# A sparse-attention and two-layer expert kernel: the experts' first layer as seven block products on two of three token chunks

## The chip, the cores and the metric

The kernel runs on one core of a Trainium2 chip. The metric is the device time of one execution in microseconds (us); the median of a few runs is quoted. A profiled execution is a run of its own, with a time of its own and a span from its first to its last instruction.

## The reference

Attention (2 batches, 8 heads, 768 positions, head size 64, each query sees 4 sink positions and a window of 128) gives 1536 tokens of 512 numbers. A first feed-forward part follows, and then four weighted experts, which are dense: every token goes through every expert.

```python
x = attention(q, k, v)                      # [1536, 512]
h = x @ w_in                                # [512, 2048]
g = np.maximum(h, 0.0) + alpha * np.minimum(h, 0.0)
y = g @ w_out                               # [2048, 512]
p = domain_probs / (domain_probs.sum(-1, keepdims=True) + 1e-09)
for e in range(4):
    h = np.maximum(y @ w1[e], 0.0)          # w1[e] [512, 1024]
    out += p[:, e:e + 1] * (h @ w2[e])      # w2[e] [1024, 512]
```

## The kernel before, in words

Every fp32 operand of the feed-forward parts is split into a high part (fp32r, what TensorE takes) and a low part (the rest), and a product is three matmuls: high by high, high by low, low by high. A matmul takes 128x128 weights and a moving tile of 512 columns.

Tokens come in three chunks `c` of 512 (`CH`). Hidden features come in f-tiles of 128: 16 of the first part (`N1`), then 8 for each expert, 48 in all (`NW`), numbered `k` or `f`. An f-tile's weights are four 128x128 blocks of the first layer and 512 columns of the second, together 1024 columns, held as `wh` (high) and `wl` (low), loaded in two halves of 512 columns into four raw buffers `wraw` and split by ScalarE (L119, high) and GpSimd or VectorE (L121, low). Eight f-tiles fit at a time: six in the pool `work`, two in the pools `late`. `tick` starts one half and takes every half that is in flight a step further; `load_due` issues the loads that have become possible.

`fast` does the attention and, woven into it, the first f-tiles. `rest` does all that follows: a list of steps (block, chunk, f-tile). In a step TensorE runs `s1` (first layer: 12 matmuls into a PSUM bank, L201 to L203), then ScalarE and VectorE make the high part `hh` and the low part `hl` of the activation (`relu`, L239 and L240), and two steps later TensorE runs the second layer for that f-tile (`s2_natural`, L219 to L221: four token tiles of three matmuls each, into four PSUM banks which add up over the 8 f-tiles of an expert). At the end of a chunk of an expert VectorE multiplies each bank by the token's share and adds it to `acc` (L669), 12 times for each expert. In the last expert, each such row of 128 tokens is sent out (L671). `y` (in `xh`, `xl`) is what the first part leaves in `acc`, split (L659, L660).

Each engine works through its queue in the order of the program, and waits on semaphores. VectorE, ScalarE and GpSimd are fed by the same loop, so what stands ahead of an instruction in this order on its engine comes first.

Of the kernel before, what the change touches and what calls it, by code (L numbers as in the profile page):

```python
# [30 lines left out]
BLOCKS = [(0, 6), (6, 5), (11, 5)] + [(N1 + 8 * e, 8) for e in range(E)]  # L31
SW = 2 * P + SK
KW = 3 * P + 2 * SK
SLOTS, EARLY, RAW = 8, 6, 4
# [18 lines left out]
class Body:  # L53
# [37 lines left out]
    def half(self, j):  # L91

        nc, (k, i) = self.nc, divmod(j, 2)
        w = self.wraw.pop(j)
        if k < N1:
            top, low = w[:, :, 1], w[:, :, 0]
            m = self.work.tile([P, CH], I32, tag="cm", name=f"cm{j}", bufs=2)  # L100
            nc.scalar.activation(m.bitcast(F32), top.bitcast(F32), AF.Abs, scale=2.0 ** -112)
            if j not in DVE_LOW:
                nc.scalar.activation(low, low.bitcast(U32), AF.Copy, scale=2.0 ** -29)
            yield
            if j in DVE_LOW:
                nc.vector.tensor_scalar(low, low.bitcast(U32), 2.0 ** -29, None, ALU.mult)
            nc.vector.tensor_scalar(top, top, -0x80000000, None, ALU.bitwise_and)  # L107
            nc.vector.scalar_tensor_tensor(top, m, 3, top, ALU.logical_shift_left, ALU.bitwise_or)
            nc.gpsimd.tensor_tensor(top, top, low, ALU.add)
            yield  # L110
            w = top.bitcast(F32)
        if i == 0:
            slot = k % SLOTS - EARLY
# [8 lines left out]
        self.due.append(j + RAW)  # L122

    def tick(self, more=True):

        if self.queue and more:
            j = self.queue.pop(0)
            self.flight.append((j, self.half(j)))
# [94 lines left out]
    def prelu(self, pool, ps, n, col, name):  # L223

        nc = self.nc
        gh = pool.tile([P, n], F32R, tag="gh", name=f"gh{name}", bufs=3)
        gl = pool.tile([P, n], F32R, tag="gl", name=f"gl{name}", bufs=3)
        g = pool.tile([P, n], F32, tag="g", name=f"g{name}", bufs=2)
# [6 lines left out]
    def relu(self, pool, ps, n, name):  # L235
        nc = self.nc
        hh = pool.tile([P, n], F32R, tag="gh", name=f"hh{name}", bufs=3)
        hl = pool.tile([P, n], F32R, tag="gl", name=f"hl{name}", bufs=3)
        nc.scalar.activation(hh, ps, AF.Relu)  # L239
        nc.vector.scalar_tensor_tensor(hl, ps, 0.0, hh.bitcast(F32), ALU.max, ALU.subtract)  # L240
        return hh, hl


    def positions(self):
# [239 lines left out]
    def ahead(self):  # L484

        self.qk, self.v, self.vs, self.sp, self.ps, self.p = {}, {}, {}, {}, {}, {}
        self.den, self.pt, self.st, self.pv, self.nmax = {}, {}, {}, {}, {}
        self.r, self.rb, self.xf = {}, {}, {}
        self.xh, self.xl, self.acc = {}, {}, {}
        self.queue, self.flight, self.due = [], [], list(range(RAW))  # L490
        for j in range(3):
            self.at_load(j)

    def fast(self):
        nc, tc = self.nc, self.tc
        self.work = accp = tc.alloc_tile_pool(name="accp", bufs=1)
        for c in range(NC):
            self.acc[c] = accp.tile([P, 4, CH], F32, name=f"acc{c}")
        tmp = tc.alloc_tile_pool(name="tmp", bufs=1)
        psb = self.psb = tc.alloc_tile_pool(name="psb", bufs=1, space=PSUM)  # L500
        with tc.tile_pool(name="psa", bufs=1, space=PSUM) as self.psa:
            at = self.at = tc.alloc_tile_pool(name="at", bufs=1)
            self.atk = tc.alloc_tile_pool(name="atk", bufs=1, side="right")
            self.late = []
            for j in range(3, QK):
# [6 lines left out]
            for i, visits in enumerate(LEAD):  # L512
                steps = [(u, f, f == f0, f == f1 - 1) for u, f0, f1 in visits for f in range(f0, f1)]
# [7 lines left out]
            gs, outs, seen = {}, None, set()  # L521
            for p in range(NP + 4):
# [56 lines left out]
                if p % 2 == 0:  # L579
                    self.at_x(p - 4)  # L580
                if p == NP + 3:
                    at.release()
                    self.add_late()
                self.tick(p in STARTS)
# [6 lines left out]
        psb.release()  # L591
        for late in self.late[::-1]:
            late.release()
        tmp.release()
        accp.release()

    def add_late(self):
# [4 lines left out]
    def rest(self, pool, units, blk0):  # L602

        nc, tc = self.nc, self.tc
        n1 = len(BLOCKS) - E
# [5 lines left out]
        nxt = SLOTS  # L611
        with tc.tile_pool(name="psc", bufs=1, space=PSUM) as psc:
            psum = [self.psb, psc]
            gs, outs = {}, None
            for i in range(len(steps) + 2):
                if i < len(steps):
                    k, c, n, f = steps[i]
                    nn = n.stop - n.start
                    self.load_due()
                    ps = psum[i % 2].tile([P, CH], F32, tag="h", name=f"h{k}_{c}_{f}", bufs=2)[:, :nn]  # L620
                    self.ready(f)
                    self.s1(f, self.xh[c][:, :, n], self.xl[c][:, :, n], ps)
                    gs[i] = (self.prelu(pool, ps, nn, f, f"{c}_{f}") if k < n1
                             else self.relu(pool, ps, nn, f"{c}_{f}"))
# [18 lines left out]
                while nxt < NW and last.get(nxt - SLOTS, -1) <= i:  # L643
                    self.plan(nxt)
                    nxt += 1
                self.tick()
                if f < f1:
                    continue
                if k == n1 - 1:
                    self.new_x(c, "y")  # L650
                for d in range(4):
                    acc = self.acc[c][:, d, n]
                    if k == 0:
                        nc.vector.tensor_copy(acc, outs[d])
                        continue
                    if k < n1:
                        nc.vector.tensor_tensor(acc, outs[d], acc, ALU.add)
                        if k == n1 - 1:
# [7 lines left out]
                    if k == n1:  # L666
                        nc.vector.tensor_scalar(acc, outs[d], pr, None, ALU.mult)
                    else:
                        nc.vector.scalar_tensor_tensor(acc, outs[d], pr, acc, ALU.mult, ALU.add)  # L669
                    if k == len(BLOCKS) - 1:  # L670
                        nc.sync.dma_start(self.a["out"][nt * P:(nt + 1) * P, :], acc)  # L671


    def general(self):
# [146 lines left out]
```

## Time and profile before

| | |
|---|---|
| median of 3 runs | 933.68 us (932.7 to 934.55) |
| the profiled execution, its own time | 937.81 us |
| its span | 936.0 us |
| TensorE matmuls | 4760, busy for 98% of the span |
| VectorE, ScalarE, GpSimd busy | 38%, 30%, 29% |
| mean granted TensorE clock | 0.987 of full speed |

Busy times of TensorE overlap, since a matmul starts before the one ahead of it has ended; how fast it goes is read from the starts. The experts' first matmul starts its weight load at 397.17 us, and the last matmul of all starts at 929.43 us.

### The profile page before, as it was taken

What the parts mean: (1) busy time and instruction counts of PE and PEld (TensorE: products, weight loads), DVE (VectorE), ACT (ScalarE), POOL (GpSimd) and SP (SyncE); (2) the same over time, 40 slices, a digit from 0 to 9 for tenths busy, and PEclk for the clock granted to TensorE, in tenths of its full rate; (3) what the DMA queues carried; (4) which work ended last, traced back from release to release, by engine and by line L of the source; (5) the groups of instructions that cost most, each with busy time, mean ns of one, the idle gap of its engine ahead of it and who ended that gap; (6) DMA issues with size and microseconds to landing.
All of it is one profiled execution on the core that took longest, in us unless ns stands there. A gap on an engine that the chain in (4) does not pass through costs nothing.

```text
span 936.0 us, 12192 instructions
## 1 busy us (share of the span) xinstructions
PE 920.7 (98%) x4760; PEld 761.3 (81%) x4760; DVE 360.2 (38%) x770; ACT 285.3 (30%) x666; POOL 276.1 (29%) x250
## 2 busy tenths in 40 slices
PE   8999999998999999999999999999999999999997
PEld 5678899998878888888888888888888888888885
DVE  5678867647994634321212122121212121212121
ACT  4687766754431222321111221112121112211110
POOL 2366644535662554551001231002230012220000
PEclk9799999998999999999999999999999999999999
DMA  6554432202331020011001120001120001101011
GB/s 181 156 180 149 149 116 86 74 1 74 130 116 43 23 68 23 23 55 36 1 0 35 46 68 34 0 1 46 50 86 0 1 19 49 57 12 46 1 46 49
DMA packets 23715, 54.44 MB, mean 58 GB/s; under 512 B 3168, under 2 KB 3168, under 8 KB 23648
## 3 DMA queue, kind: packets, MB, share of 16 engines
q1 hardware_dynamic: 23504, 53.57, 17.7%
q8 instruction: 39, 0.64, 0.3%
q14 instruction: 28, 0.23, 0.1%
q10 hardware_dynamic: 144, 0.00, 0.0%
HBM read 50.42 MB, written 3.15 MB: 57 GB/s over the span
## 4 chain that ended last, share of the span: by engine, by line
PE 90%; DVE 7%; ACT 1%; issue 1%; POOL 0%; ACTq 0%; DVEq 0%; POOLq 0%
PE h L201 13%; PE h L202 13%; PE h L203 13%; PE o L221 9%; PE o L220 9%; PE o L219 9%; PE o L210 4%; PE o L211 4%; PE o L212 4%; PE pv L455 3%; PE s L348 2%; PE pt L408 2%; PE busy L184 1%; DVE wraw L107 1%; DVE wl L121 1%
## 5 line engine op out<-in xcount | busy, mean ns | idle before, releaser
L240 DVE SCALAR_TENSOR_TENSOR hl<-h,hh 128x512 fp32r<-128x512 f32 x96 | 66.4, 692 | 428.7 <-ACT hh L239 428.7
L121 POOL TENSOR_TENSOR wl<-wraw,wh 128x512 fp32r<-128x512 f32 x79 | 103.4, 1313 | 362.0 <-ACT wh L119 362.0
L239 ACT ACTIVATE hh<-h 128x512 fp32r<-128x512 f32 x96 | 57.4, 598 | 428.4 <-PE h L203 428.4
L202 PE MATMUL h<-yl,wh 128*128 128x512 f32 x384 | 150.2, 391 | 0.0
L221 PE MATMUL o<-wh,hl 128*128 128x512 f32 x384 | 150.2, 391 | 0.0
L201 PE MATMUL h<-yh,wh 128*128 128x512 f32 x384 | 150.2, 391 | 0.0
L219 PE MATMUL o<-wh,hh 128*128 128x512 f32 x384 | 150.0, 391 | 0.0
L220 PE MATMUL o<-wl,hh 128*128 128x512 f32 x384 | 150.0, 391 | 0.0
L203 PE MATMUL h<-yh,wl 128*128 128x512 f32 x384 | 149.8, 390 | 0.0
L201 PE MATMUL h<-xh,wh 128*128 128x256 f32 (+1 forms) x264 | 90.7, 344 | 0.0
L203 PE MATMUL h<-xh,wl 128*128 128x256 f32 (+1 forms) x264 | 88.3, 334 | 0.0
L202 PE MATMUL h<-xl,wh 128*128 128x256 f32 (+1 forms) x264 | 88.2, 334 | 0.0
L201 PEld LDWEIGHTS h<-yh,wh 128*128 128x128 f32 x384 | 72.0, 188 | 15.9
L203 PEld LDWEIGHTS h<-yh,wl 128*128 128x128 f32 x384 | 72.1, 188 | 15.8
L202 PEld LDWEIGHTS h<-yl,wh 128*128 128x128 f32 x384 | 72.1, 188 | 15.8
L221 PEld LDWEIGHTS o<-wh,hl 128*128 128x128 f32 x384 | 72.1, 188 | 15.6
L219 PEld LDWEIGHTS o<-wh,hh 128*128 128x128 f32 x384 | 72.1, 188 | 15.6
L220 PEld LDWEIGHTS o<-wl,hh 128*128 128x128 f32 x384 | 72.1, 188 | 15.4
L232 POOL TENSOR_TENSOR gl<-g,gh 128x512 fp32r<-128x512 f32 (+1 forms) x36 | 48.2, 1339 | 80.7 <-ACT gh L231 80.6
L119 ACT ACTIVATE wh<-wraw 128x512 fp32r<-128x512 f32 x96 | 60.0, 636 | 9.3 <-PE o L221 6.5
L231 ACT ACTIVATE gh<-g 128x512 fp32r<-128x512 f32 (+1 forms) x36 | 21.5, 597 | 126.4 <-DVE g L230 126.4
L210 PE MATMUL o<-gh,wh 128*128 128x512 f32 (+1 forms) x144 | 55.0, 382 | 4.3 <-ACT gh L231 2.5
(96 smaller groups left out, 1397.5 us busy)
## 6 DMA issues: line engine op xcount, KB each, us to landing
wraw<-in_w SPq DMA_DIRECT2D x32, 512.0 KB, 3.7
wraw<-in_w SPq DMA_DIRECT2D x64, 256.0 KB, 2.5
qk<-in_qk SPq DMA_DIRECT2D x21, 352.0 KB, 3.0
v<-in_v SPq DMA_DIRECT2D x12, 256.0 KB, 3.3
out<-acc SPq DMA_DIRECT2D x12, 256.0 KB, 2.0
qk<-in_qk SPq DMA_DIRECT2D x8, 272.0 KB, 3.2
qk<-in_qk SPq DMA_DIRECT2D x11, 176.0 KB, 3.1
qk<-in_qk SPq DMA_DIRECT2D x8, 136.0 KB, 3.3
```

Source lines behind the costliest of these rows:

```text
L119: nc.scalar.activation(hi, w, AF.Copy)
L121: eng.tensor_tensor(lo, w, hi.bitcast(F32), ALU.subtract)
L201: mm(ps, wh[:, c], xh[:, dk, :], start=dk == 0, stop=False)
L202: mm(ps, wh[:, c], xl[:, dk, :], start=False, stop=False)
L203: mm(ps, wl[:, c], xh[:, dk, :], start=False, stop=dk == DM // P - 1)
L210: mm(outs[dt], wh[:, c], gh, start=first and begins[dt], stop=False, skip_group_check=True)
L219: mm(outs[nt], hh[:, c], wh[:, CH:], start=first, stop=False)
L220: mm(outs[nt], hh[:, c], wl[:, CH:], start=False, stop=False)
L221: mm(outs[nt], hl[:, c], wh[:, CH:], start=False, stop=last)
L232: nc.gpsimd.tensor_tensor(gl, g, gh.bitcast(F32), ALU.subtract)
L239: nc.scalar.activation(hh, ps, AF.Relu)
L240: nc.vector.scalar_tensor_tensor(hl, ps, 0.0, hh.bitcast(F32), ALU.max, ALU.subtract)
```

## The change

On chunks 0 and 1 together, the first layer of a pair of f-tiles is a product of 2x2 blocks: (two chunks x two halves of the 512 features) by (two halves of the features x two f-tiles). Eight block products make it up. The change forms it from seven, by Winograd's form of Strassen's scheme: sums of blocks of `y` (`sums`, once for all experts) and of the weights (`pair`, for each pair of f-tiles) are made first, and the seven products are combined by five additions on VectorE (`four`). Chunk 2 stays with `s1`. The first pair of the first expert is still done by the loop of `rest`, the other 15 pairs by `experts`. In these, the second layer adds up in PSUM over the two f-tiles of a pair alone, one token tile after the other (`out`), and VectorE adds each to `acc`. The work on the first part of the feed-forward is as before, but for deeper buffers of its activations and other places for some temporary tiles.

```diff
-BLOCKS = [(0, 6), (6, 5), (11, 5)] + [(N1 + 8 * e, 8) for e in range(E)]
+BLOCKS = [(0, 6), (6, 5), (11, 5), (N1, 2)]
+PAIR1 = N1 + 2
...
+    def pair(self, j):
...
+        def split(hi, lo, x):
+            nc.scalar.activation(hi, x, AF.Copy)
+            nc.gpsimd.tensor_tensor(lo, x, hi.bitcast(F32), ALU.subtract)
+        def part(i):
+            c = slice(i % 2 * CH, (i % 2 + 1) * CH)
+            split(self.wh[k + i // 2][:, c], self.wl[k + i // 2][:, c], w[i])
...
+        part(0)
+        yield
+        part(2)
+        yield
...
+        minus(t[0][:, :UN], b12, b11)
+        minus(t[0][:, UN:], b22, t[0][:, :UN])
+        yield
+        minus(t[1][:, :UN], b22, b12)
+        minus(t[1][:, UN:], b21, t[0][:, UN:])
+        self.due += [j + RAW, j + RAW + 2]
+        yield
+        part(1)
+        self.due.append(j + RAW + 1)
+        yield
+        part(3)
+        self.due.append(j + RAW + 3)
+        yield
...
+        split(th[:, :CH], tl[:, :CH], t[0])
+        yield
+        split(th[:, CH:], tl[:, CH:], t[1])
...
     def prelu(self, pool, ps, n, col, name):
-        gh = pool.tile([P, n], F32R, tag="gh", name=f"gh{name}", bufs=3)
+        wide = pool is self.wide
+        gh = pool.tile([P, n], F32R, tag="gh", name=f"gh{name}", bufs=6 if wide else 3)
...
+    def relu_hi(self, h, name):
...
+        self.nc.scalar.activation(hh, h, AF.Relu)
+    def relu_lo(self, h, parts):
+        hh, hl = parts
+        self.nc.vector.scalar_tensor_tensor(hl, h, 0.0, hh.bitcast(F32), ALU.max, ALU.subtract)
...
+    def sums(self):
...
+        for d in range(2):
+            nc.vector.tensor_tensor(one[d], b[:, d, :], b[:, 2 + d, :], ALU.add)
+            nc.vector.tensor_tensor(t, one[d], a[:, d, :], ALU.subtract)
+            split(2, d, t, nc.gpsimd)
+            yield
+            nc.vector.tensor_tensor(u, a[:, 2 + d, :], t, ALU.subtract)
+            split(4, d, u, nc.gpsimd)
+            yield
+            nc.vector.tensor_tensor(t, a[:, d, :], b[:, d, :], ALU.subtract)
+            split(3, d, t, nc.gpsimd)
+            yield
+        self.sh[1], self.sl[1] = self.xh[1][:, :2, :], self.xl[1][:, :2, :]
+        for d in range(2):
+            split(1, d, one[d], nc.vector)
...
+    def four(self, k):
+        while any(j <= 2 * k for j in self.queue + [j for j, _ in self.flight]):
+            self.load_due()
+            self.tick()
...
+        product(p[0], A[11], B[11], True)
+        nc.scalar.activation(p1, p[0], AF.Copy)
+        product(p[1], S[2], T[1], True)
+        add(u2, p[1], p1)
+        product(p[2], S[3], T[2], True)
+        add(u3, p[2], u2)
+        product(p[3], S[1], T[0], True)
+        add(c22, p[3], u3)
+        h22 = self.relu_hi(c22, f"{k}_22")
+        product(p[0], A[12], B[21], False)
+        h11 = self.relu_hi(p[0], f"{k}_11")
+        self.relu_lo(c22, h22)
+        self.relu_lo(p[0], h11)
+        product(p[2], A[22], T[3], False)
+        add(c21, p[2], u2)
+        h21 = self.relu_hi(c21, f"{k}_21")
+        product(p[3], S[4], B[22], False)
+        add(c12, p[3], u2)
+        h12 = self.relu_hi(c12, f"{k}_12")
+        self.later = [lambda: self.relu_lo(c21, h21), lambda: self.relu_lo(c12, h12)]
+        self.hid[k] = [(h11, h12), (h21, h22)]
+    def out(self, k, c, hid):
+        for d in range(CH // P):
+            ps = self.psum[1].tile([P, CH], F32, tag="o", name=f"o{k}_{c}_{d}", bufs=2)
+            n = slice(d * P, (d + 1) * P)
+            for x, (hh, hl) in enumerate(hid):
+                wh, wl = self.wh[k + x][:, CH:], self.wl[k + x][:, CH:]
+                mm(ps, hh[:, n], wh, start=x == 0, stop=False)
+                mm(ps, hh[:, n], wl, start=False, stop=False)
+                mm(ps, hl[:, n], wh, start=False, stop=x == 1)
...
+            nc.vector.scalar_tensor_tensor(acc, ps, self.prob[:, nt, e:e + 1], acc, ALU.mult, ALU.add)
+            self.leave(1)
+            if d % 2:
+                self.load_due()
+                self.tick()
+            if k == NW - 2:
+                nc.sync.dma_start(self.a["out"][nt * P:(nt + 1) * P, :], acc)
+    def leave(self, n=None):
+        for step in self.later[:n]:
+            step()
+        del self.later[:n]
+    def experts(self):
+        last = None
+        for k in range(PAIR1, NW, 2):
+            if k > PAIR1:
+                self.four(k)
+            if last:
+                self.out(k - 2, 2, last)
+            if k + 4 < NW:
+                self.queue.append(2 * (k + 4))
+            last = []
+            for x in range(2):
+                ps = self.psum[0].tile([P, CH], F32, tag="o", name=f"h{k}_c{x}", bufs=2)
+                self.s1(k + x, self.xh[2], self.xl[2], ps)
+                last.append(self.relu(ps, f"{k}_c{x}"))
+            self.load_due()
+            self.tick()
+            self.leave()
+            for c in range(2):
+                self.out(k, c, self.hid[k][c])
+        self.out(NW - 2, 2, last)
...
     def rest(self, pool, units, blk0):
+                if i == len(steps):
+                    self.four(PAIR1)
+                self.leave()
...
+                if (k, c) in [(n1 - 1, 2), (n1, 0), (n1, 1)] and (c, f) != (1, N1 + 1):
+                    next(sums, None)
```

`product(ps, a, b, first)` is six matmuls: for each of two 128-row slices, high by high, low by high, high by low. `A` are blocks of `y`, `S` sums of them, `B` blocks of the weights, `T` sums of those (`th`, `tl`, in the two `late` pools). `u2`, `u3`, `p1`, `c22`, `c21`, `c12` are fp32 tiles of 128x512 in SBUF. `minus` is a subtraction of 128x256 on GpSimd.

## Rows read from the trace of the kernel before

**Rows 1.** The page, part 4: the chain that ended last, by engine.

```profile
PE 90%; DVE 7%; ACT 1%; issue 1%; POOL 0%; ACTq 0%; DVEq 0%; POOLq 0%
```

**Rows 2.** Busy time by stretch: stretch, length, PE, PEld, DVE, ACT, POOL, clock, DMA.

```profile
397.17:410.93 13.76, 13.76 (x61) 11.25 (x60) 3.77 (x6) 5.18 (x10) 7.50 (x6) 1.00 0.18 58
410.93:929.90 518.97, 518.90 (x2270) 425.66 (x2268) 96.15 (x142) 84.11 (x147) 70.86 (x56) 1.00 0.09 30
```

**Rows 3.** Timeline of weight loads: start, us, instruction; runs of twelve matmuls begin here.

```profile
602.83 0.19 PEld L219 LDWEIGHTS o<-wh,hh 128*128 128x128 f32 x1
...
605.55 0.19 PEld L201 LDWEIGHTS h<-yh,wh 128*128 128x128 f32 x1
...
608.35 0.19 PEld L219 LDWEIGHTS o<-wh,hh 128*128 128x128 f32 x1
```

**Rows 4.** Groups of the experts' stage: busy us, mean ns, idle before; L240: minimum/median/maximum ns.

```profile
L202 PE MATMUL h<-yl,wh 128*128 128x512 f32 x384 | 150.2, 391 | 0.0
L121 POOL TENSOR_TENSOR wl<-wraw,wh 128x512 fp32r<-128x512 f32 x56 | 72.1, 1294 | 355.0 <-ACT wh L119 355.0
L119 ACT ACTIVATE wh<-wraw 128x512 fp32r<-128x512 f32 x56 | 34.0, 624 | 6.5 <-PE o L221 6.5
L669 DVE SCALAR_TENSOR_TENSOR acc<-o,prob,acc 128x512 f32<-128x512 f32 x36 | 24.6, 743 | 4.9 <-PE o L221 4.9
...
L240 DVE SCALAR_TENSOR_TENSOR hl<-h,hh x96: 691/692/694, 401.0 to 922.2; 128x512 fp32r<-128x512 f32 x96
```

**Rows 5.** DMA issues: KB each, median us to landing; whole run, and its end.

```profile
wraw<-in_w SPq DMA_DIRECT2D x64, 256.0 KB, 2.5
...
out<-acc SPq DMA_DIRECT2D x12, 256.0 KB, 2.0
...
out<-acc SPq DMA_DIRECT2D x4, 256.0 KB, 3.8
```

**Rows 6.** Timeline near the end: a bank's last matmul and VectorE's start on it.

```profile
927.33 0.40 PE L221 MATMUL o<-wh,hl 128*128 128x512 f32 x1
...
927.76 2.85 DVE L669 SCALAR_TENSOR_TENSOR acc<-o,prob,acc 128x512 f32<-128x512 f32 x4 [4.90 <-PE o L221]
```

**Rows 7.** Timeline: VectorE instructions with two SBUF inputs beside GpSimd, three places.

```profile
76.01 0.42 DVE L325 TENSOR_TENSOR qs<-qk,qs 64x256 fp32r<-64x256 f32 x1
...
76.03 1.00 POOL L478 TENSOR_TENSOR xl<-xf,xh 128x256 fp32r<-128x256 f32 x1 [0.20 <-ACT xh L477]
...
233.99 0.74 POOL L232 TENSOR_TENSOR gl<-g,gh 128x256 fp32r<-128x256 f32 x1 [2.06 <-ACT gh L231]
...
234.04 1.24 DVE L108 SCALAR_TENSOR_TENSOR wraw<-cm,wraw 128x512 int32<-128x512 int32 x1
...
270.69 1.46 POOL L232 TENSOR_TENSOR gl<-g,gh 128x512 fp32r<-128x512 f32 x1
...
271.04 1.65 DVE L108 SCALAR_TENSOR_TENSOR wraw<-cm,wraw 128x512 int32<-128x512 int32 x1
272.62 1.87 DVE L657 TENSOR_TENSOR acc<-o,acc 128x512 f32<-128x512 f32 x3
...
273.44 0.47 PE L210 MATMUL o<-gh,wh 128*128 128x512 f32 x1 [1.84 <-DVE acc L657]
```

**Rows 8.** Timeline: handing over from VectorE to ScalarE, within ScalarE, and to GpSimd.

```profile
396.54 0.63 ACT L231 ACTIVATE gh<-g 128x512 fp32r<-128x512 f32 x1 [4.37 <-DVE g L230]
...
397.08 0.61 ACT L119 ACTIVATE wh<-wraw 128x512 fp32r<-128x512 f32 x1
...
397.25 1.29 POOL L232 TENSOR_TENSOR gl<-g,gh 128x512 fp32r<-128x512 f32 x1 [2.98 <-ACT gh L231]
...
407.14 2.48 DVE L657 TENSOR_TENSOR acc<-o,acc 128x512 f32<-128x512 f32 x4
...
407.86 2.43 ACT L659 ACTIVATE yh<-acc 128x512 fp32r<-128x512 f32 x4 [0.84 <-DVE acc L657]
```

**Rows 9.** A stretch with TensorE's wait of 273.44 in it: PE, clock, DMA.

```profile
272.00:275.00 3.00, 1.56 (x7) 1.00 0.46 165
```

More of the change, by code (lines that the diff above doesn't have):

```diff
@@ L112, in half @@
         if i == 0:
-            slot = k % SLOTS - EARLY
+            slot = k % SLOTS - EARLY if k < N1 else -1
             pool, n = (self.work, EARLY) if slot < 0 else (self.late[slot], 1)
@@ L122, in half, with minus @@
         self.due.append(j + RAW)
+    def pair(self, j):
+        nc, k = self.nc, j // 2
+        w = [self.wraw.pop(j + i) for i in range(4)]
+        for x in (k, k + 1):
+            self.wh[x] = self.work.tile([P, 2 * CH], F32R, tag="wh", name=f"wh{x}", bufs=EARLY)
+            self.wl[x] = self.work.tile([P, 2 * CH], F32R, tag="wl", name=f"wl{x}", bufs=EARLY)
+        def split(hi, lo, x):
[4 more added lines that the diff above has]
+            split(self.wh[k + i // 2][:, c], self.wl[k + i // 2][:, c], w[i])
+        def minus(out, a, b):
+            nc.gpsimd.tensor_tensor(out, a, b, ALU.subtract)
+        part(0)
+        yield
+        part(2)
+        yield
+        b11, b21, b12, b22 = w[0][:, :UN], w[0][:, UN:], w[2][:, :UN], w[2][:, UN:]
+        t = [self.work.tile([P, CH], I32, tag="cm", name=f"t{j}_{i}", bufs=2).bitcast(F32) for i in range(2)]
+        minus(t[0][:, :UN], b12, b11)
[11 more added lines that the diff above has]
+        yield
+        late = self.late[k // 2 % 2]
+        th = self.th[k] = late.tile([P, 2 * CH], F32R, tag="wh", name=f"th{k}", bufs=1)
+        tl = self.tl[k] = late.tile([P, 2 * CH], F32R, tag="wl", name=f"tl{k}", bufs=1)
+        split(th[:, :CH], tl[:, :CH], t[0])
+        yield
+        split(th[:, CH:], tl[:, CH:], t[1])
     def tick(self, more=True):
         if self.queue and more:
-            j = self.queue.pop(0)
-            self.flight.append((j, self.half(j)))
+            j = self.queue[0]
+            if j < 2 * PAIR1 or all(j + i in self.wraw for i in range(4)):
+                self.queue.pop(0)
+                self.flight.append((j, self.half(j) if j < 2 * PAIR1 else self.pair(j)))
         for g in self.flight[::-1]:
@@ L225, in prelu @@
         nc = self.nc
-        gh = pool.tile([P, n], F32R, tag="gh", name=f"gh{name}", bufs=3)
-        gl = pool.tile([P, n], F32R, tag="gl", name=f"gl{name}", bufs=3)
-        g = pool.tile([P, n], F32, tag="g", name=f"g{name}", bufs=2)
+        wide = pool is self.wide
+        gh = pool.tile([P, n], F32R, tag="gh", name=f"gh{name}", bufs=6 if wide else 3)
+        gl = pool.tile([P, n], F32R, tag="gl", name=f"gl{name}", bufs=6 if wide else 3)
+        if wide:
+            g = self.qks[self.turns % 2][:, :n]
+            self.turns += 1
+        else:
+            g = pool.tile([P, n], F32, tag="g", name=f"g{name}", bufs=2)
         nc.vector.tensor_scalar(g, ps, 0.0, self.alpha[:, col:col + 1], ALU.min, ALU.mult)
@@ L233, in prelu @@
         return gh, gl
[L235 to L240, printed above, removed]
-        return hh, hl
+    def relu_hi(self, h, name):
+        hh = self.wide.tile([P, CH], F32R, tag="gh", name=f"hh{name}", bufs=6)
+        hl = self.wide.tile([P, CH], F32R, tag="gl", name=f"hl{name}", bufs=6)
+        self.nc.scalar.activation(hh, h, AF.Relu)
+        return hh, hl
@@ new lines, in relu_lo, with relu, split @@
+    def relu_lo(self, h, parts):
+        hh, hl = parts
+        self.nc.vector.scalar_tensor_tensor(hl, h, 0.0, hh.bitcast(F32), ALU.max, ALU.subtract)
+    def relu(self, h, name):
+        parts = self.relu_hi(h, name)
+        self.relu_lo(h, parts)
+        return parts
+    def sums(self):
+        nc, (a, b) = self.nc, (self.acc[0], self.acc[1])
+        def split(i, d, x, eng):
+            hi, lo = self.sh[i][:, d, :], self.sl[i][:, d, :]
+            nc.scalar.activation(hi, x, AF.Copy)
+            eng.tensor_tensor(lo, x, hi.bitcast(F32), ALU.subtract)
+        one = [self.raws[d][:, CH:] for d in range(2)]
+        t, u = [self.raws[2 + d][:, CH:] for d in range(2)]
+        for d in range(2):
[12 more added lines that the diff above has]
+            split(1, d, one[d], nc.vector)
+        yield
@@ new lines, in four, with product, add @@
+    def four(self, k):
+        nc, mm = self.nc, self.nc.tensor.matmul
+        while any(j <= 2 * k for j in self.queue + [j for j, _ in self.flight]):
+            self.load_due()
+            self.tick()
+        xh, xl, (w, v) = self.xh, self.xl, (k, k + 1)
+        low, high = slice(0, UN), slice(UN, CH)
+        B = {11: (w, low), 21: (w, high), 12: (v, low), 22: (v, high)}
+        B = {i: (self.wh[x][:, c], self.wl[x][:, c]) for i, (x, c) in B.items()}
+        T = [(self.th[k][:, i * UN:(i + 1) * UN], self.tl[k][:, i * UN:(i + 1) * UN]) for i in range(4)]
+        A = {11: (xh[0][:, :2, :], xl[0][:, :2, :]), 12: (xh[0][:, 2:, :], xl[0][:, 2:, :]),
+             22: (xh[1][:, 2:, :], xl[1][:, 2:, :])}
+        S = {i: (self.sh[i], self.sl[i]) for i in range(1, 5)}
+        def product(ps, a, b, first):
+            (ah, al), (bh, bl) = a, b
+            for d in range(2):
+                c = slice(d * P, (d + 1) * P)
+                mm(ps, bh[:, c], ah[:, d, :], start=first and d == 0, stop=False, skip_group_check=True)
+                mm(ps, bh[:, c], al[:, d, :], start=False, stop=False, skip_group_check=True)
+                mm(ps, bl[:, c], ah[:, d, :], start=False, stop=d == 1, skip_group_check=True)
+        p = [self.psum[i // 2].tile([P, CH], F32, tag="h", name=f"h{k}_{i}", bufs=2) for i in range(4)]
+        p1, u2, u3, c22 = [self.raws[i][:, CH:] for i in range(4)]
+        c21, c12 = [self.qks[2 + i][:, :CH] for i in range(2)]
+        def add(out, a, b):
+            nc.vector.tensor_tensor(out, a, b, ALU.add)
+        product(p[0], A[11], B[11], True)
[19 more added lines that the diff above has]
+        self.hid[k] = [(h11, h12), (h21, h22)]
@@ new lines, in out @@
+    def out(self, k, c, hid):
+        nc, mm, e = self.nc, self.nc.tensor.matmul, (k - N1) * P // F2
+        for d in range(CH // P):
[6 more added lines that the diff above has]
+                mm(ps, hl[:, n], wh, start=False, stop=x == 1)
+            nt = c * (CH // P) + d
+            acc = self.acc[c][:, d, :]
+            nc.vector.scalar_tensor_tensor(acc, ps, self.prob[:, nt, e:e + 1], acc, ALU.mult, ALU.add)
[5 more added lines that the diff above has]
+                nc.sync.dma_start(self.a["out"][nt * P:(nt + 1) * P, :], acc)
@@ L490, in ahead @@
         self.queue, self.flight, self.due = [], [], list(range(RAW))
+        self.sh, self.sl, self.th, self.tl, self.hid, self.later = {}, {}, {}, {}, {}, []
+        self.wide, self.turns = None, 0
         for j in range(3):
@@ L502, in fast @@
             at = self.at = tc.alloc_tile_pool(name="at", bufs=1)
+            tmp = tc.alloc_tile_pool(name="tmp", bufs=1)
             self.atk = tc.alloc_tile_pool(name="atk", bufs=1, side="right")
@@ L581, in fast @@
                 if p == NP + 3:
+                    tmp.release()
                     at.release()
@@ L593, in fast @@
             late.release()
-        tmp.release()
         accp.release()
@@ L604, in rest @@
         nc, tc = self.nc, self.tc
-        n1 = len(BLOCKS) - E
+        n1 = len(BLOCKS) - 1
         steps = [(0, u // 2, slice(u % 2 * UN, (u % 2 + 1) * UN), f) for u in units for f in range(BLOCKS[0][1])]
@@ L611, in rest @@
         nxt = SLOTS
+        self.wide = pool
+        for i in (2, 3, 4):
+            self.sh[i] = pool.tile([P, 2, CH], F32R, name=f"s{i}h")
+            self.sl[i] = pool.tile([P, 2, CH], F32R, name=f"s{i}l")
+        sums = self.sums()
         with tc.tile_pool(name="psc", bufs=1, space=PSUM) as psc:
-            psum = [self.psb, psc]
+            psum = self.psum = [self.psb, psc]
             gs, outs = {}, None
@@ L622, in rest @@
                     self.s1(f, self.xh[c][:, :, n], self.xl[c][:, :, n], ps)
-                    gs[i] = (self.prelu(pool, ps, nn, f, f"{c}_{f}") if k < n1
-                             else self.relu(pool, ps, nn, f"{c}_{f}"))
+                    gs[i] = self.prelu(pool, ps, nn, f, f"{c}_{f}") if k < n1 else self.relu(ps, f"{c}_{f}")
                     for s in steps[i + 1:i + 2]:
                         self.ready(s[3])
+                if i == len(steps):
+                    self.four(PAIR1)
+                self.leave()
                 i -= 2
@@ L642, in rest @@
                     self.s2_natural(f, gh, gl, outs, f == f0, f == f1)
-                while nxt < NW and last.get(nxt - SLOTS, -1) <= i:
+                while nxt < PAIR1 and last.get(nxt - SLOTS, -1) <= i:
                     self.plan(nxt)
                     nxt += 1
+                while PAIR1 <= nxt < PAIR1 + 4 and last[nxt + 1 - SLOTS] <= i:
+                    self.queue.append(2 * nxt)
+                    nxt += 2
                 self.tick()
+                if (k, c) in [(n1 - 1, 2), (n1, 0), (n1, 1)] and (c, f) != (1, N1 + 1):
+                    next(sums, None)
                 if f < f1:
@@ L665, in rest @@
                     pr = self.prob[:, nt, k - n1:k - n1 + 1]
[L666 to L671, printed above, removed]
+                    nc.vector.tensor_scalar(acc, outs[d], pr, None, ALU.mult)
+            self.experts()
     def general(self):
```

1 line of the change is left out of this document (removed).

## The prediction

> **What bounds the kernel now.** I read the chain of waits first: 90% of the span hangs on TensorE itself [rows 1]. Then the busy times by stretch, for the experts' stage alone: TensorE is busy for all of it at a granted clock of 1.00, while VectorE works 96 of 519 us, ScalarE 84 and GpSimd 71 [rows 2]. So in this stage time is the number of matmuls by the distance between their starts. Third, the starts themselves. Twelve matmuls of a second-layer step take 605.55 - 602.83 = 2.72 us, those of the next first-layer step 2.80 [rows 3]: 0.2267 or 0.2333 us for one. Why there are two rates the rows don't say. Over the stage, from 397.17 [rows 2] to the last start at 929.43 plus one interval, there are 6 x 384 = 2304 matmuls [rows 4] and 24 that the two-step lag leaves over from the first part: 532.5 / 2328 = 0.2287 us each.
>
> **What is removed.** A pair of f-tiles takes 2 x 2 x 12 = 48 first-layer matmuls on chunks 0 and 1 before, and seven products of six, 42, after. Fifteen pairs save 90 matmuls: 90 x 0.2287 = 20.6 us. The second layer and chunk 2 keep their matmuls. The new operands lie elsewhere, so the rate may move: if all 2214 matmuls left ran at 0.2267 the stage's 2304 x 0.2287 = 526.9 us would fall by 25.0, at 0.2333 by 10.4. I keep 0.2287, since both kinds of place stay in use.
>
> **What is added off TensorE.** A pair lasts (42 + 24 + 72) x 0.2287 = 31.6 us. In it VectorE now has 12 accumulations of 0.743, five additions of some 0.7 (an estimate from L669 and L240) and six low parts of 0.692, in all 16.6 us; ScalarE one copy, six activations and six splits of some 0.62, 8 us; GpSimd six splits of 1.294 and four subtractions of half the width (at most as much each), 8 to 13 us [rows 4]. None of them fills the 31.6 us. The weights of a pair are four loads that land in 2.5 us [rows 5], issued at least one step ahead of their splits; the splits and sums of pair k+4 start when pair k's chunk 2 is done and end in pair k+2, before `four(k+4)` asks for them, so its loop at the head finds nothing to wait for. SP's queue holds only these loads until the last pair. The sums of `y` are ten VectorE instructions, eight ScalarE copies and six GpSimd subtractions over seven steps of 24 x 0.2287 = 5.5 us, where activations are used two steps after they start: hidden, cost 0; were that cover gone, 1.1 us for each of them that meets GpSimd would be the bound, some 8 us.
>
> **Where a wait can arise.** In `out` a token tile has six matmuls, 1.37 us, in one of two banks. TensorE can begin tile d+2 when VectorE has added tile d. VectorE starts 927.76 - 927.33 = 0.43 us after the start of a bank's last matmul [rows 6], which is 0.20 us after the next tile could start; it takes 0.743 [rows 4], and TensorE follows an evacuation 273.44 - 272.62 = 0.82 us after the start of a 0.68 us one, so 0.14 behind its end [rows 7]. That is 1.08 us of the 1.37: no wait, if VectorE is free. It holds for `out` on chunks 0 and 1. In `out(k-2, 2)`, straight after `four(k)`, two low parts stand in VectorE's queue, for c21 behind tile 0 and for c12 behind tile 1, and both read two SBUF tensors. GpSimd splits `part(3)` and `th` of pair k+2 there, because ScalarE comes to their high parts when h12 is done.
>
> What happens when such two meet, the trace shows. At 234.04 VectorE's L108, 0.69 us where it runs alone, started 0.05 us behind a GpSimd subtraction and took 1.24, ending 0.55 behind the end of that one; at 271.04 it took 1.65 and ended 0.54 behind; the evacuation queued behind it came late and TensorE stood for 1.84 us. At 76.01 VectorE was first by 0.02 us and was not slowed; GpSimd's 256 columns took 1.00 instead of 0.74 [rows 7]. Low parts with one input in PSUM never vary, 691 to 694 ns over the stage [rows 4].
>
> The Trainium skill says the same of this (SBUF — State Buffer, section "Who interferes with whom"): a VectorE instruction with two SBUF inputs and a GpSimd instruction that reads SBUF exclude each other, and the one that starts first keeps the other out until it is done. The trace agrees, with 0.05 us of a lead on one side and 0.02 on the other deciding. By the rule the change puts such a meeting into each pair, and the sum below has it; without the rule and the rows it would end at -20.6.
>
> So who is first? Count from the start of c12's addition, 0.43 us behind the start of the last matmul of `four`. ScalarE follows an addition of this kind 407.86 - 407.14 = 0.72 us after its start and starts the next instruction 0.54 later; that lasts some 0.62, and GpSimd is 0.08 behind its end [rows 8]: GpSimd starts at 0.72 + 0.54 + 0.62 + 0.08 = 1.96. VectorE: tile 0 ends 6 x 0.2267 = 1.36 us later, the accumulation takes 0.743, and the next instruction starts some 0.07 before the end (272.62 against 271.04 + 1.65 [rows 7]): 2.03. GpSimd is first by 0.07 us. It holds the port until 1.96 + 1.29 = 3.25, c21's low part ends at 3.25 + 0.54 = 3.79, the accumulation of tile 1 ends at 3.79 - 0.07 + 0.74 = 4.46, and TensorE may begin tile 3 at 4.60. It would have begun at 19 x 0.2267 - 0.43 = 3.88. The wait is 0.72 us. c12's low part is then held in the same way, but the tiles behind it are the last two and the next user of their banks comes 5.5 us later. Fourteen pairs have `out(k-2, 2)` behind `four`: 14 x 0.72 = 10.1 us. If VectorE is first it is free at 2.72, tile 3's bank at 3.60, and the cost is 0. A wait of 0.7 us is not charged to the clock: it stayed 1.00 in this kernel in the stretch with the one of 1.84 us [rows 9].
>
> **At the ends.** The first matmul of `experts` takes a bank of `rest`'s last chunk, which VectorE is just emptying: 0 to 0.74, I take 0.3. The last four rows of the output were sent 0.70 us apart and landed in 3.8 us, others in 2.0 [rows 5, 6]; now they come 1.37 apart: 0 to 1.8 us saved, I take 0.9.
>
> **Sum**, against the profiled execution: 937.8 - 20.6 + 10.1 + 0.3 - 0.9 = 926.7. That execution was 4.1 us over the median of the runs shown, so the median is forecast at 922.6, which is 1.2% faster.
>
> **Rivals.** *VectorE wins the race to the port*, so nothing waits: 933.7 - 20.6 + 0.3 - 0.9 = 912.5. For it: the lead of 0.07 us is a sum of five durations, and with the slower rate of [rows 3] VectorE comes 0.04 later still, which speaks against it. *Some of the pairs lose it, some don't*: about 917. *The stage's rate goes to 0.2333*, with the port lost: 922.6 + 14.6 = 937, slower; with it won, 927. *On the other side*: the two banks of `out`. Before, a bank had 24 matmuls, now it is emptied every 1.37 us, 180 times. My 1.08 us leaves 0.29 of slack. Each 0.1 us by which emptying took longer than 1.37 would cost 18 us, so the change is a loss from 1.49 us on for one emptying (11 us gone to the port taken as well: from 1.43 on). Against it: the 0.43, 0.743 and 0.14 are all read from this kernel and vary little. *The change doesn't do what it says*, since the products wait for VectorE's additions: each accumulating product comes at least 12 matmuls, 2.7 us, behind the first use of its bank, and the addition between takes 0.43 + 0.7; no change would need 1.4 us of waiting in each pair.
>
> **Numbers.** Port lost in nearly every pair 0.55, port won 0.24, mixed 0.12, slower by banks or rate 0.05, eaten up by waits 0.04. 0.2% either way (1.9 us) is what a measurement of this kernel can tell. The range goes from the port won with a little of the faster rate, 910.5, to the port lost with a third of the way to the slower rate, 927.5. Faster 0.92, same 0.03, slower 0.05.
>
> **What the profile would show.** Matmuls 4670, starts still 0.227 to 0.233 apart, clock 1.00. In the waits, TensorE behind L669's successor in `out`, about 14 times, some 0.7 us each, always at the fourth token tile of chunk 2; the low part of c21 taking about 1.7 us instead of 0.69 there, beside a GpSimd split that began just before it. If no such waits appear, VectorE's low part is short and GpSimd's split some 0.5 us long instead. I am wrong if TensorE stands at the head of `four` (weights late), between its products, or at every tile of `out`, or if the starts lie elsewhere than 0.2267 to 0.2333.

## The result and the profile after

The changed kernel takes 927.17 us (median of 5 runs, 923.67 to 927.71) against 933.68 (5 runs, 932.7 to 937.88): a ratio of 0.9916, 95% interval 0.9887 to 0.9946, so 0.8% faster. Forecast were 922.6 and 910.5 to 927.5. The profiled execution took 927.69 us with a span of 925.5; the sum had been made for such an execution and gave 926.7.

Runs of one and the same kernel differ by up to 9.6 us here (929.01 to 938.65 for the kernel before, over all its runs), and the level goes with TensorE's mean clock, which was or was not at half level for a while in the first 230 us (last section). The experiments are therefore compared by the experts' *stage* too, from the first weight load of the experts to the last one of all; there the clock was 1.00 in every trace. The kernel before needs 929.20 - 397.17 = 532.03 us for 2328 matmuls, the changed one 919.57 - 396.66 = 522.91 for 2238.

The page of the changed kernel: busy times, and the chain that ended last, by engine.

```profile
PE 903.0 (98%) x4670; PEld 742.2 (80%) x4670; DVE 549.3 (59%) x999; ACT 316.2 (34%) x719; POOL 371.6 (40%) x346
PE 85%; DVE 12%; issue 1%; ACT 1%; POOL 0%; DVEq 0%; ACTq 0%; POOLq 0%
```

There are 90 matmuls fewer, and the chain runs through VectorE for 12% of the span, where it was 7% [rows 1]. What TensorE (PE) and its weight loads (PEld) waited for in the stage: us in all, times, longest.

```profile
PE o L395 <- DVE acc L400: 6.2, 13, 0.5
PE o L268 <- DVE acc L871: 1.1, 1, 1.1
PE h_c L250 <- DVE acc L871: 0.2, 1, 0.2
...
PEld o L395 <- DVE acc L400: 11.7, 13, 0.9
```

Thirteen waits in `out`, one in `rest`'s last part, one short one at the head of `experts`. One of the thirteen, in order of time (start, us, engine, line):

```profile
537.60 0.69 DVE L363 TENSOR_TENSOR qk<-h,wraw 128x512 f32<-128x512 f32 x1 [0.70 <-PE h L356]
...
538.86 0.62 ACT L135 ACTIVATE wh<-wraw 128x512 fp32r<-128x512 f32 x1
538.96 0.75 DVE L400 SCALAR_TENSOR_TENSOR acc<-o,prob,acc 128x512 f32<-128x512 f32 x1 [0.67 <-PE o L397]
...
539.56 1.30 POOL L136 TENSOR_TENSOR wl<-wraw,wh 128x512 fp32r<-128x512 f32 x1 [13.36 <-ACT wh L135]
539.63 1.77 DVE L297 SCALAR_TENSOR_TENSOR hl<-qk,hh 128x512 fp32r<-128x512 f32 x1
...
540.82 1.72 POOL L136 TENSOR_TENSOR tl<-t,th 128x512 fp32r<-128x512 f32 x1
...
541.26 0.39 PE L397 MATMUL o<-wh,hl_c 128*128 128x512 f32 x1
541.33 0.74 DVE L400 SCALAR_TENSOR_TENSOR acc<-o,prob,acc 128x512 f32<-128x512 f32 x1
541.99 1.10 DVE L297 SCALAR_TENSOR_TENSOR hl<-qk,hh 128x512 fp32r<-128x512 f32 x1
542.12 0.19 PEld L395 LDWEIGHTS o<-wh,hh_c 128*128 128x128 f32 x1 [0.90 <-DVE acc L400]
542.12 0.50 PE L395 MATMUL o<-wh,hh_c 128*128 128x512 f32 x1 [0.48 <-DVE acc L400]
```

From c12's addition (537.60) GpSimd's split starts 1.96 us later, VectorE's low part 2.03: the two numbers of the forecast, to the hundredth. GpSimd is ahead by 0.07; the low part takes 1.77 instead of 0.69 and ends at 541.40, 0.54 behind the end of the split, as in [rows 7]. The accumulation of the second token tile is late, and TensorE begins the fourth 1.09 us after its last weight load at 541.03 instead of 0.23. (`hl<-qk,hh` is the low part of c21 or c12.)

The wait that was not foreseen, from the timeline of the same kernel:

```profile
417.88 1.14 ACT L313 ACTIVATE yh<-wraw 128x512 fp32r<-128x512 f32 x2
418.39 1.30 POOL L136 TENSOR_TENSOR wl<-wraw,wh 128x512 fp32r<-128x512 f32 x1
418.54 3.40 DVE L314 TENSOR_TENSOR yl<-wraw,yh 128x512 fp32r<-128x512 f32 x2 [0.87 <-ACT yh L313]
419.65 1.74 POOL L136 TENSOR_TENSOR tl<-t,th 128x512 fp32r<-128x512 f32 x1
...
421.86 2.71 DVE L871 TENSOR_SCALAR acc<-o,prob 128x512 f32<-128x512 f32 x4
...
422.74 0.47 PE L268 MATMUL o<-wh,hh 128*128 128x512 f32 x1 [1.06 <-DVE acc L871]
```

The last step of `sums` puts its two subtractions on VectorE. They start behind GpSimd's split of a weight, meet two of them and take 3.40 us for two; the four evacuations of `rest` behind them are late, and TensorE stands.

### The profile page after: what moved, and what is told of

Same layout as the page of the kernel before. It is cut to its first block, busy times and chain, and to the rows that moved or that the text cites. A ratio compares the mean times of both kernels' runs of the same rounds, so it can differ in the third digit from the quotient of the medians.

```text
span 925.5 us, 12401 instructions
## 1 busy us (share of the span) xinstructions
PE 903.0 (98%) x4670; PEld 742.2 (80%) x4670; DVE 549.3 (59%) x999; ACT 316.2 (34%) x719; POOL 371.6 (40%) x346
## 4 chain that ended last, share of the span: by engine, by line
PE 85%; DVE 12%; issue 1%; ACT 1%; POOL 0%; DVEq 0%; ACTq 0%; POOLq 0%
PE o L395 8%; PE o L397 8%; PE o L396 8%; PE h L354 5%; PE h L356 5%; PE h L355 5%; PE h L250 4%; PE h L251 4%; PE h L252 4%; PE o L259 4%; PE o L260 4%; PE o L261 4%; PE pv L646 3%; PE h_c L250 3%; PE h_c L251 3%; PE h_c L252 3%
## 5 line engine op out<-in xcount | busy, mean ns | idle before, releaser
L400 DVE SCALAR_TENSOR_TENSOR acc<-o,prob,acc 128x512 f32<-128x512 f32 x180 | 134.8, 749 | 77.4 <-PE o L397 76.5
L395 PE MATMUL o<-wh,hh 128*128 128x512 f32 x240 | 93.4, 389 | 0.0
L396 PE MATMUL o<-wl,hh 128*128 128x512 f32 x240 | 93.4, 389 | 0.0
L397 PE MATMUL o<-wh,hl 128*128 128x512 f32 x240 | 93.4, 389 | 0.0
L286 POOL TENSOR_TENSOR gl<-qk,gh 128x512 fp32r<-128x512 f32 (+1 forms) x36 | 49.2, 1369 | 77.8 <-ACT gh L285 75.5
L250 PEld LDWEIGHTS h<-xh,wh 128*128 128x128 f32 x264 | 50.1, 190 | 6.6 <-issue 1.7
L260 PE MATMUL o<-gl,wh 128*128 128x512 f32 (+1 forms) x144 | 54.5, 378 | 0.5 <-POOL gl L286 0.5
L261 PE MATMUL o<-gh,wl 128*128 128x512 f32 (+1 forms) x144 | 54.3, 377 | 0.0
L252 PEld LDWEIGHTS h<-xh,wl 128*128 128x128 f32 x264 | 50.0, 189 | 5.3 <-DVE wl L122 0.3
L251 PEld LDWEIGHTS h<-xl,wh 128*128 128x128 f32 x264 | 50.1, 190 | 4.9
```

The lines of the kernel that those rows point to most:

```text
L250: mm(ps, wh[:, c], xh[:, dk, :], start=dk == 0, stop=False)
L251: mm(ps, wh[:, c], xl[:, dk, :], start=False, stop=False)
L252: mm(ps, wl[:, c], xh[:, dk, :], start=False, stop=dk == DM // P - 1)
L260: mm(outs[dt], wh[:, c], gl, start=False, stop=False, skip_group_check=True)
L261: mm(outs[dt], wl[:, c], gh, start=False, stop=last, skip_group_check=True)
L395: mm(ps, hh[:, n], wh, start=x == 0, stop=False)
```

## The experiments

Each kernel ran beside the kernel before on the same chip, three chips in all (the first four, the next three, the last two; the kernel before had medians of 933.53, 937.26 and 937.0 there). Ratios are to the kernel before, with 95% intervals. The medians also contain what the clock did ahead of the stage: the four runs of e3_banks had a mean clock of 0.994 to 0.999, those of e6_sums 0.987 to 0.993, so e3_banks has the lower median and e6_sums the shorter stage.

| kernel | median us | ratio | stage us (matmuls) |
|---|---|---|---|
| before | 933.68 | 1 | 532.03 (2328) |
| after | 927.17 | 0.9916 [0.9887, 0.9946] | 522.91 (2238) |
| e1_apart | 916.41 | 0.983 [0.9792, 0.9867] | 512.44 (2238) |
| e2_pause | 915.39 | 0.9833 [0.9795, 0.9872] | 513.20 (2238) |
| e3_banks | 910.41 | 0.9784 [0.9743, 0.9824] | 512.45 (2238) |
| e4_eight | 931.68 | 0.9981 [0.9956, 1.0005] | 528.18 (2328) |
| e5_low | 913.46 | 0.9742 [0.9711, 0.9774] | 512.44 (2238) |
| e6_sums | 914.88 | 0.9765 [0.9736, 0.9793] | 511.08 (2238) |
| e7_all | 914.63 | 0.9764 [0.974, 0.9788] | 511.08 (2238) |
| e8_line | 909.77 | 0.9721 [0.9676, 0.9766] | 507.52 (2238) |
| e9_before_line | 929.16 | 0.9944 [0.9914, 0.9974] | 527.46 (2328) |

**e1_apart: the weight splits leave `out` on chunk 2.** The steps of the weights are taken at the token tiles of chunks 0 and 1 instead, as many of them, where no low part of c21 or c12 is queued.

```diff
-            if d % 2:
+            if c == 1 or c == 0 and d % 2:
                 self.load_due()
                 self.tick()
```

> The two weight steps that fell into out(k-2, 2) are moved ahead, into out(k, 1): a step after every token tile there, none on chunk 2. Same work on every engine. Theory (VectorE's low part of c21 is kept out by GpSimd's subtraction): GpSimd is idle in that place, the low part takes 0.69 us, and TensorE's 13 waits with their 0.80 us each are gone: 10.4 us less than the changed kernel, some 917 us. Rival (the two low parts cost the wait by standing in VectorE's queue between the accumulations, whoever else works): the waits stay, 927 us.

All thirteen waits are gone. The thirty low parts, by group (busy, mean ns), in the changed kernel and then in this one:

```profile
L297 DVE SCALAR_TENSOR_TENSOR hl<-qk,hh 128x512 fp32r<-128x512 f32 x30 | 40.1, 1336 | 0.1
```

```profile
L297 DVE SCALAR_TENSOR_TENSOR hl<-qk,hh 128x512 fp32r<-128x512 f32 x30 | 20.5, 682 | 0.1
```

So the low part was long by the split beside it, and by nothing else; the stage lost 10.47 us.

**e2_pause: the same instructions in the same order, only GpSimd later.** A copy of 256 columns on ScalarE, into a tile that nobody reads, stands ahead of the split `part(3)`. It takes 0.40 us and so turns the lead of 0.07 round.

```diff
+        pause = self.wide.tile([P, UN], F32, tag="pause", name=f"pause{j}", bufs=1)
+        nc.scalar.activation(pause, w[3][:, :UN], AF.Copy)
         part(3)
```

> Work is added: a copy of 256 columns on ScalarE ahead of part(3), 15 times, so that GpSimd starts its subtraction some 0.3 us later. Theory (who is first at the port decides, by 0.07 us): VectorE is now first by about 0.25 us, its low part of c21 takes 0.69 us, GpSimd's subtraction some 1.7, and the 13 waits are gone: some 917 us. Rival (the two engines slow each other by the amount of work that overlaps, in whatever order): no better than 927 us.

Two meetings in this run's timeline; in the first TensorE's next tile is shown too (the lines of the file are two further down here):

```profile
469.48 2.99 POOL L136 TENSOR_TENSOR wl<-wraw,wh 128x512 fp32r<-128x512 f32 x2 [11.81 <-ACT wh L135]
...
469.56 1.77 DVE L299 SCALAR_TENSOR_TENSOR hl<-qk,hh 128x512 fp32r<-128x512 f32 x1
...
472.05 0.50 PE L397 MATMUL o<-wh,hh_c 128*128 128x512 f32 x1 [0.48 <-DVE acc L402]
...
501.85 0.68 DVE L299 SCALAR_TENSOR_TENSOR hl<-qk,hh 128x512 fp32r<-128x512 f32 x1
...
502.08 1.61 POOL L136 TENSOR_TENSOR wl<-wraw,wh 128x512 fp32r<-128x512 f32 x1 [12.46 <-ACT wh L135]
```

At 501.85 VectorE is first by 0.23: its low part takes 0.68, GpSimd's split 1.61 instead of 1.30, and no tile is late. At 469.5, the one place of this kind in the run, another half's copy stands on ScalarE ahead of the pause (it starts at 468.79, the pause at 469.31), GpSimd is first by 0.08, and the wait of `out` is there. The kernel gains 9.7 us of stage by an instruction more in each pair: who starts first decides, and not that the two overlap, which they do at 501.85 as well.

**e3_banks: the meeting stays, the tile behind it gets room.** `out` takes its banks in turn from both PSUM pools, four banks for two.

```diff
-            ps = self.psum[1].tile([P, CH], F32, tag="o", name=f"o{k}_{c}_{d}", bufs=2)
+            ps = self.psum[1 - d % 2].tile([P, CH], F32, tag="o", name=f"o{k}_{c}_{d}", bufs=2)
```

> out() takes its PSUM banks by turns from both pools, so four of them rotate instead of two; nothing else changes, the steps stay where they meet. Theory (the port delays VectorE, and two banks turn that into a wait of TensorE): the low part of c21 still takes some 1.77 us, but TensorE does not wait: some 917 us. Rival (TensorE is held up by something else in this place, operands or the weights): the waits stay, 927 us.

GpSimd and VectorE meet as before, in this run's timeline:

```profile
498.15 1.30 POOL L136 TENSOR_TENSOR wl<-wraw,wh 128x512 fp32r<-128x512 f32 x1 [12.12 <-ACT wh L135]
...
498.23 1.77 DVE L297 SCALAR_TENSOR_TENSOR hl<-qk,hh 128x512 fp32r<-128x512 f32 x1
```

Yet TensorE waits nowhere in `out`, and the stage is 512.45, as in e1_apart. The slow low part costs only through the bank that it keeps occupied.

**e4_eight: the second layer per pair alone.** The first layer of a pair is done with eight block products by `s1`, without `sums`, T weights and additions; `out` and its accumulations are those of the changed kernel.

```diff
-        product(p[0], A[11], B[11], True)
...
-        add(c12, p[3], u2)
...
+        self.hid[k], n = [[], []], 0
+        for c in range(2):
+            for x in range(2):
+                ps = self.psum[n // 2].tile([P, CH], F32, tag="h", name=f"h{k}_{n}", bufs=2)
...
+                self.s1(k + x, self.xh[c], self.xl[c], ps)
+                self.hid[k][c].append(self.relu(ps, f"{k}_{c}{x}"))
```

> The second layer per pair and token tile alone: four() does the eight block products as four calls of s1 with the activation straight from PSUM; no sums of y, no sums of weights. 90 matmuls come back, 20.6 us; no VectorE instruction of out() reads two SBUF tensors any more. Theory: no waits at all, so 927.2 + 20.6 - 12.2 (all of the changed kernel's waits) = some 935.5 us, the kernel before within 0.3%: the new order of the second layer costs and brings nothing by itself. Rival (emptying a bank every six matmuls is what makes TensorE wait): 945 us or more.

No wait but the one at the head of `experts` (0.85 us between two weight loads instead of 0.23): emptying a bank every 1.36 us costs nothing. The stage is 3.85 us shorter than that of the kernel before, which was not expected. All its matmuls but the 24 left over from the first part start 0.2267 us apart, where the kernel before has 0.2286 on average; that is where the 3.85 us come from, after the 0.62 are paid. Here every f-tile of the experts lies in `work`, in the kernel before two of eight lie in `late`. So the next runs ask what is slow about `late`.

**e5_low: the late pools 16 KB lower.** The weights `th` and `tl` lie in the pools `late`, at the top of the memory. On e3_banks, the four raw buffers are put at the top and the late pools move below them.

```diff
-        self.raws = [self.base.tile([P, 2 * CH], F32, name=f"wraw{i}") for i in range(RAW)]
+        top = ctx.enter_context(tc.tile_pool(name="top", bufs=1, side="right"))
+        self.raws = [top.tile([P, 2 * CH], F32, name=f"wraw{i}") for i in range(RAW)]
```

> On top of the four rotating banks: the raw weight buffers, which TensorE does not read in the experts' stage, change places in SBUF with the two late pools, which hold the sums of weights and lay at the top of the partitions. Theory (operands in the late pools make a matmul start every 0.2333 us instead of 0.2267, by where they lie): the products with sums of weights go to 0.2267, the stage from its first to its last weight load falls from 512.45 to some 509 us. Rival (these products are slower because of their order or their sharing of a bank): 512.4 us again.

Nothing moves: 512.44 us, and the 360 matmuls on `th` and `tl` still start 0.2333 us apart. How high the tiles lie is not the cause.

**e6_sums: on e3_banks, the last step of `sums` a step later.**

```diff
-                if (k, c) in [(n1 - 1, 2), (n1, 0), (n1, 1)] and (c, f) != (1, N1 + 1):
+                if (k, c) in [(n1 - 1, 2), (n1, 0), (n1, 1)] and (c, f) not in [(0, N1 + 1), (1, N1 + 1)]:
```

> On top of the four rotating banks: the last step of the sums of y, two subtractions on VectorE with two SBUF inputs each, is taken one step later, where no evacuation stands behind it. Theory (these two, kept out by GpSimd, make VectorE late for the banks of the experts' first block): the single wait of 1.4 us ahead of the experts' second-layer step is gone, the stage falls from 512.45 to some 511 us. Rival (VectorE is late there from the activations anyway): the wait stays.

VectorE in this run: the evacuations first, then the subtractions.

```profile
416.69 2.72 DVE L871 TENSOR_SCALAR acc<-o,prob 128x512 f32<-128x512 f32 x4
...
423.08 2.55 DVE L314 TENSOR_TENSOR yl<-wraw,yh 128x512 fp32r<-128x512 f32 x2 [0.86 <-ACT yh L313]
```

The wait at L268 is gone and the stage is 1.37 us shorter than in e3_banks.

**e7_all: e5_low and e6_sums together.**

> Rotating banks, late pools lower, last step of the sums later, all three: the stage at some 507.6 us, the run some 905 to 909 us, 2.5 to 3% below the kernel before. If one of the three does not do what its own run says, it is missing here too.

511.08 us, as e6_sums, and not the 507.6 expected: the two edits don't touch each other, and e5_low's does nothing here either.

**e8_line: on e6_sums, 480 bytes reserved at the top.** In the compiled program the tiles of the late pools begin 32 bytes past a multiple of 64 (`wh6` at 221,152); all others of the weights at multiples of 512, as are `y`, its sums and the activations. With 480 bytes reserved above them, `wh6` begins at 220,672, a multiple of 512.

```diff
+        ctx.enter_context(tc.tile_pool(name="edge", bufs=1, side="right")).tile([P, 120], F32, name="edge")
```

> On top of the rotating banks and the later last step of the sums: 480 bytes are reserved at the top of each partition, so that the tiles of the late pools begin at multiples of 512 bytes, as all the others do; until now they began 32 bytes behind a multiple of 64. Theory (a matmul with an operand that begins there starts the next one 6.6 ns later, whatever its place otherwise): the products with sums of weights go from 0.2333 to 0.2267 us, the stage from 511.08 to some 508 us. Rival (it is the late pools' far place in SBUF, or the order of the products): 511.1 us again.

Six weight loads on T weights and the next, first in the changed kernel, then here:

```profile
534.38 0.19 PEld L354 LDWEIGHTS h<-yh,th 128*128 128x128 f32 x1
...
535.78 0.19 PEld L354 LDWEIGHTS h<-s4h,wh 128*128 128x128 f32 x1
...
537.17 0.19 PEld L395 LDWEIGHTS o<-wh,hh_c 128*128 128x128 f32 x1
```

```profile
521.11 0.19 PEld L355 LDWEIGHTS h<-yh,th 128*128 128x128 f32 x1
...
522.47 0.19 PEld L355 LDWEIGHTS h<-yh,wh 128*128 128x128 f32 x1
```

1.40 us, 0.2333 for one, become 1.36, 0.2267. Over the stage the mean of the 360 on `th` and `tl` falls from 0.2333 in e6_sums to 0.2267, which is 2.4 us; the others, some of which still ran slowly just behind one of those (the 1.39 us above for s4's six), fall from 0.2273 to 0.2267, 1.1 us. Together that is, but for rounding, the 3.56 us between 511.08 and 507.52. This is the fastest kernel of the study, 2.8% below the kernel before.

**e9_before_line: the same line in the kernel before.**

> The kernel before with the same 480 bytes reserved and nothing else. Theory (start address): its two f-tiles of eight that lie in the late pools go from 0.2333 to 0.2267, the stage from 532.03 us to some 527.8. Rival (place or order): 532.0 again.

The stage goes from 532.03 to 527.46 us, and its matmuls start 0.2267 us apart without exception. The two slow f-tiles of every eight were those in the late pools. Between the two kernels with this line, e9 and e8, lie 19.94 us of stage: 90 matmuls of 0.2267 are 20.4, less 0.55 for the wait at the head of `experts`, which leaves 19.9.

## Why the prediction was right, and where it was off

The terms of the sum against the two profiled executions, us:

| term | forecast | measured |
|---|---|---|
| 90 matmuls fewer | -20.6 | -20.6 |
| rate of the rest (0.2282 where no wait, for 0.2286) | 0 | -0.9 |
| port waits in `out(k-2, 2)` | 14 x 0.72 = 10.1 | 13 x 0.805 = 10.5 |
| `sums` | 0 | 1.4 |
| head of `experts` (0.77 us between two weight loads, for 0.23) | 0.3 | 0.5 |
| after the last weight load | -0.9 | 5.93 - 6.80 = -0.9 |
| ahead of the stage | 0 | -0.5 |
| sum | -11.1 | -10.5 |

The spans differ by 936.0 - 925.5 = 10.5, the times by 937.81 - 927.69 = 10.1.

- **The port.** Right in each of its steps: place, order, lead, length, and the 0.54 us by which the loser ends later. e1, e2 and e3 each take away one link (the meeting, its order, the bank behind it), and each gives back the same 10 us. The rule of the Trainium skill (SBUF — State Buffer, "Who interferes with whom"), that the one who starts first keeps the other out, agrees with both meetings of e2_pause, 0.08 us of a lead on the one side and 0.23 on the other. The loser ends behind the winner by 0.14 to 0.15 us less than its own length: 0.54 for VectorE's 0.69, 1.16 for GpSimd's 1.30 (503.69 against 502.53 in e2_pause). Thirteen pairs, not fourteen: pair 46 has no pair ahead whose weights are split there. Each wait is 0.80 us by e1's stage (10.47 / 13), 0.08 more than worked out: the fourth tile begins 4.52 us after c12's addition (542.12 - 537.60), 0.08 sooner than the 4.60 of the forecast, but its first matmul takes 0.50 us, others 0.39, and the second starts 0.34 us behind it (542.46) instead of 0.23.
- **The sums of `y`,** "hidden, cost 0; were that cover gone, 1.1 us for each of them that meets GpSimd": the cover was gone for the last step, whose two subtractions stand straight ahead of four evacuations. 1.06 us of waiting, 1.37 by e6_sums.
- **From the profiled execution to the median.** This was the largest error. "That execution was 4.1 us over the median of the runs shown, so the median is forecast at 922.6" takes the 4.1 for a property of the profiled run. The changed kernel's profiled run was only 0.5 over its own median. Of the 4.6 us between 922.6 and 927.17 this makes 3.6, the terms 1.0 (0.4 of it between span and time). At a mean clock of 0.988 the kernel before took 937.0 to 938.65 us (14 runs) and the changed one 926.8 to 927.69 (3 runs): 9.3 to 11.9 apart, as the sum has it. The medians show 6.5, since four of the five runs after had a clock of 0.988 or 0.989, and four of the five before took 932.7 to 934.55, which other runs of it took at 0.992 to 0.995.
- **The range held by luck.** Its upper end, "the port lost with a third of the way to the slower rate, 927.5", is 922.6 plus a third of 14.6. But 14.6 us lie between the faster rate and the slower one (25.0 - 10.4); from the 0.2287 of the sum to the slower rate it is 20.6 - 10.4 = 10.2. So the upper end should have been 926.0, below the 927.17 measured, and the rival of the slower rate 932.8 and 922.7 instead of 937 and 927. The rate, which that end was meant to allow for, went the other way (0.2282); what carried the median up there was mostly the clock of the runs (3.6 of 4.6 us, above).
- **The rivals.** "VectorE wins the race to the port", forecast at 912.5, is what e2_pause made but for one pair: 915.39 (the clock of its four runs was 0.989 to 0.995). The two banks: e4_eight shows that emptying one each 1.36 us costs nothing, as argued. "Why there are two rates the rows don't say": e8 and e9 say it.

## What to carry to other kernels

When work is moved so that VectorE, with two operands in SBUF, and GpSimd come to one place, work out who starts first, to a few hundredths of a microsecond (0.07 decided here), and see whose bank is behind the loser: a second pair of banks or another place for the split gives all of it back. Two distances between matmul starts in one trace are worth a look at where the operands begin. And a sum made against one profiled execution is carried to a median by runs at the same clock, not by that execution's distance from its median.

## What the runs showed of the hardware that was not expected

**Where an operand begins sets the rate.** Matmuls of 128x128 by 512 with an operand that begins 32 bytes past a multiple of 64 start 0.2333 us apart, with the weights too at multiples of 512, as all other operands of the stage are, 0.2267 (e8). It holds for such an operand as weights and as the moving tile: in the kernel before, the twelve matmuls of f-tile 22 take 2.80 us in the first layer (429.97 to 432.77) and as much in the second (443.73 to 446.53), those of an f-tile in `work` 2.72. Some matmuls just behind slow ones are slow too (the 1.39 us above). Only these two offsets were run, so where between them the effect begins is open.

**Half clock early in some runs.** Windows of three runs: the kernel before, the changed one, e3_banks; the clock is the number behind POOL's, then DMA share and GB/s.

```profile
18.00:24.00 6.00, 4.79 (x27) 2.77 (x28) 4.96 (x16) 3.27 (x12) 3.05 (x3) 1.00 0.60 201
24.00:30.00 6.00, 6.00 (x19) 3.33 (x20) 3.67 (x14) 2.31 (x7) 2.65 (x3) 0.53 0.65 198
```

```profile
18.00:24.00 6.00, 4.33 (x19) 2.36 (x17) 5.62 (x17) 3.20 (x13) 3.01 (x3) 0.86 0.47 147
24.00:30.00 6.00, 6.00 (x19) 3.26 (x19) 3.09 (x11) 1.84 (x7) 2.11 (x3) 0.50 0.63 195
```

```profile
18.00:24.00 6.00, 4.79 (x27) 2.61 (x26) 4.62 (x17) 3.27 (x11) 2.54 (x4) 1.00 0.45 132
24.00:30.00 6.00, 4.95 (x24) 2.75 (x24) 5.31 (x17) 3.25 (x12) 3.08 (x4) 1.00 0.88 260
```

In the kernel before the clock falls to half, 1.2 of 2.4 GHz, after a stretch in which TensorE worked 4.79 of 6 us; in e3_banks it worked 4.79 there as well, and the clock stayed. (In the changed kernel the fall, at 22.3 us, lies inside the first window.) The edit of e3_banks touches no instruction of this stretch, and the kernel before has runs of both kinds. Why some executions fall and others don't was not settled. In all nine traces with this fall the clock is at half once more near 220 us. What both cost shows in where the experts' stage begins: at 388.38 us in e3_banks, whose clock stays at 1.00, and at 396.66, 8.28 us later, in the changed kernel, which has the same instructions ahead of it. The mean clock over the run tells the executions apart: for the kernel before 0.999 in runs of 929.01 to 929.94 us, 0.988 in those of 937.0 to 938.65.
